# Attention and mixer on one core: the first channel product of two more chunks by seven half-size products, the last stores in more pieces, and every job in a new order

## The chip, the core and the metric

The kernel runs on one core of a Trainium2 chip. The core has five engines, each with its own queue of instructions: TensorE (PE in the profile, with PEld for its weight loads) for matrix products, VectorE (DVE) and ScalarE (ACT) for work on vectors, GpSimd (POOL), and SyncE (SP), which here only issues DMAs. Engines wait for each other through semaphores. The metric is device time in microseconds, the median of the runs; lower is better.

## The reference

`q`, `k` and `v` have 8 batch entries, 8 heads, 576 positions and head size 64. Linear attention with 128 random features gives `x`, and a token mixer and a channel mixer follow:

```python
def phi(x):                      # x: q or k, scaled by 64 ** -0.25
    proj = np.einsum('bhsd,md->bhsm', x, omega)
    h = proj - np.sum(x * x, axis=-1, keepdims=True) / 2.0
    h = h - np.max(h, axis=-1, keepdims=True)
    return np.exp(h) / np.sqrt(m)
q_p, k_p = phi(q_s), phi(k_s)
kv = np.einsum('bhsm,bhsd->bhmd', k_p, v);  z = np.sum(k_p, axis=2)
x = einsum('bhsm,bhmd->bhsd', q_p, kv) / (einsum('bhsm,bhm->bhs', q_p, z)[..., None] + 1e-06)
# x becomes [8, 576, 512]
h = np.maximum(x.transpose(0, 2, 1) @ w_tok1, 0.0) @ w_tok2     # 576 -> 256 -> 576
u = x + h.transpose(0, 2, 1)
out = u + np.maximum(u @ w_ch1, 0.0) @ w_ch2                    # 512 -> 1536 -> 512, float32
```

## The kernel before

A chunk is one batch entry's first 512 positions; chunks are numbered 0 to 7. The last 64 positions of all eight entries are gathered into a ninth chunk, number 8. Each chunk goes through three stages:

- `attention(b)`: products of the keys and queries with `omega` (lines 594 to 714), their exponentials on ACT (`exp`, line 557), row maxima of the keys on DVE (`km`, line 735), `v` scaled by their reciprocals (`vs_`, recorded at line 338), and two products with 65 columns (lines 758 and 791), whose result is divided and written to `x` (lines 807 and 809).
- `token_mix(b)`: two products (lines 826 and 839), the sum `u`, and a DMA on SP that transposes `u` into `uT` (line 847).
- `channel_mix(c)`: a first product with `wc1` and a rectifier into `r3` (tile `r`), then a second with `wc2`, added to `u` and stored.

The channel products are 512 by 512 by 1536. The second is done, from chunk 1 on, by `channel_out_fast`: both operands are cut in two by two blocks, and seven half-size products replace eight (products of block sums, put together again by additions). The block sums of `r3` go into tile `S`, those of the weights into `T`; the results are read out of the banks by `read` (line 964). The first is done in this way by `channel_in_fast` for the chunks from `FAST_IN` on: 4 to 8 here. For chunks below that, `channel_mix` runs 12 plain products of four matmuls of 512 columns (line 1167), each followed by a rectifier out of its bank.

In `channel_in_fast` each of three groups (`m`) has seven products of four matmuls of 256 columns (line 1096), P1 to P7. Three intermediate results are copied out of the banks (`keep`, ACT, recorded at line 329), three times DVE adds a kept copy to a bank (`join`, line 1120), and rectifiers follow: one out of a bank and two in place in SBUF. Four block differences of `uT` and eight sums of weights (`weight_sums`, once for the kernel) are needed as well. All sums can run on DVE or POOL.

The order of work is set by hand-held tables. Every piece of work is a job with a number, and `Planner.run` issues the jobs in the order of the list `ORDER` (a negative entry is a matmul on zeros that keeps the array busy). `SLOT` says which buffer of a ring each job takes, and `MOVED` on which engine a job runs where that isn't the usual one. An engine runs its own jobs strictly in that order. Between DVE and POOL, jobs marked `port` from attention chunk 2 on wait for the other engine's last such job (`Planner.turns`): the later one of a pair starts only after the earlier.

Keys and queries of chunks 2 to 7 are cast to half precision by POOL's DMAs into a scratch in DRAM, and then read back transposed by DMAs on SP (`load_transposed`, line 423). SP's queue also holds the transposes of `u` and many of the stores.

Of the kernel before, what the change touches and what calls it, by code (L numbers as in the profile page):

```python
# [208 lines left out]
def kernel(  # L209
# [12 lines left out]
    nc = tc.nc  # L222
# [3 lines left out]
    DM = H * D  # L226
# [8 lines left out]
    NCB = DC // P  # L235
    NU = H // 2
    R = SM // 2
    RT = ST // 2
    RA = R + RT
    NPE = 2  # L240
    FAST_IN = 4
    SPLIT = ()
    HALVES = ()
    RW = S * 4 // P
    c_scale = float(1.0 / math.sqrt(math.sqrt(D)))

    pool = ctx.enter_context(tc.tile_pool(name="sb", bufs=1))
# [1027 lines left out]
```

## Time and profile before

| | us |
|---|---|
| median of 3 runs (lowest, highest) | 272.78 (272.64, 273.68) |
| profiled execution, first to last instruction | 271.2 |
| PE busy, of that span | 262.6 (97%) |
| DVE busy | 225.1 (83%) |
| ACT busy | 167.4 (62%) |
| POOL busy | 149.9 (55%) |

The profiled execution has no other time of its own than its span; the median of the runs is 1.58 us above that span, which is what lies before the first and behind the last recorded instruction. The profile page shows busy time for each engine, the chain of work that ended last, and groups of instructions by source line. "L1167" is line 1167 of the kernel; `bank<-uT,wc` means that the instruction reads tiles `uT` and `wc` and writes a PSUM bank. Where a helper records the operation (lines 329 to 338), one line stands for many jobs, and the tiles tell them apart. Matmuls are pipelined, so the time of one is longer than the step from one to the next; the step is read from the chain, where so many matmuls fill so many microseconds.

### The profile page before, as it was taken

Reading aid. Unit: us, or ns where it says so; the run is one execution under the profiler, and the core shown is the slowest. Engines: PE = TensorE matmul, PEld = TensorE weight load, DVE = VectorE, ACT = ScalarE, POOL = GpSimd, SP = SyncE. Lnnn points to the kernel's source line nnn. Section 1 sums busy time; section 2 is a strip of 40 time slices with the busy share of each in tenths; the row PEclk is TensorE's granted clock in tenths of the full one; section 3 lists DMA queues with packets and bytes.
Section 4 is the critical chain, followed back from the end, with each engine's and each line's share of the span. In section 5 each row is a group of like instructions: output and inputs, shape, how many; then the busy total and the mean of one; then the engine's idle time right before and its main releaser. Section 6 shows DMA issues by size and latency. Waiting matters only on the chain.

```text
span 271.2 us, 6792 instructions
## 1 busy us (share of the span) xinstructions
PE 262.6 (97%) x2683; PEld 183.9 (68%) x2683; DVE 225.1 (83%) x483; ACT 167.4 (62%) x395; POOL 149.9 (55%) x155
## 2 busy tenths in 40 slices
PE   8899999999999999999999999999999999999992
PEld 4457455444557655775468687886698688888882
DVE  3888879759879779988888989989987986899882
ACT  2999942179683639637965989777768342482400
POOL 8895393066882694662898893692551025404041
PEclk9999999999999999999999999999999999999998
DMA  7999999998999999999846999701160182030026
GB/s 195 191 208 210 191 211 183 192 217 148 196 234 172 251 219 150 163 236 192 163 91 103 214 130 221 187 2 77 39 139 2 21 155 81 2 155 2 19 87 209
DMA packets 81297, 39.72 MB, mean 146 GB/s; under 512 B 63984, under 2 KB 77040, under 8 KB 81072
## 3 DMA queue, kind: packets, MB, share of 16 engines
q0 software_dynamic: 31744, 17.74, 44.1%
q1 hardware_dynamic: 46928, 15.37, 28.5%
q10 hardware_dynamic: 2592, 6.16, 6.0%
q8 instruction: 21, 0.34, 0.5%
q14 instruction: 12, 0.10, 0.1%
HBM read 35.95 MB, written 16.52 MB: 193 GB/s over the span
## 4 chain that ended last, share of the span: by engine, by line
PE 91%; ACT 3%; DMA 3%; DVE 1%; issue 0%
PE bank L984 27%; PE bank L1096 16%; PE bank L1167 15%; PE bank L826 5%; PE bank L839 5%; PE bank L1201 4%; PE bank L791 3%; PE bank L702 3%; PE bank L758 3%; DMA kT<-k 3%; PE bank L714 2%; PE bank L1241 1%; ACT kp L557 1%; PE bank L513 1%; PE bank L793 1%; PE bank L819 1%
## 5 line engine op out<-in xcount | busy, mean ns | idle before, releaser
L338 POOL TENSOR_TENSOR vs<-v,vs 128x512 f16<-128x512 f16 x31 | 32.7, 1060 | 24.4 <-DVE vs L739 9.6
L1167 PE MATMUL bank<-uT,wc 128*128 128x512 f16 x184 | 44.1, 379 | 0.0
L557 ACT ACTIVATE kp<-bank 128x512 f16<-128x512 f32 x64 | 34.9, 617 | 14.5 <-PE bank L702 14.5
L333 ACT ACTIVATE r<-bank 128x512 f16<-128x512 f32 (+1 forms) x52 | 30.6, 607 | 19.4 <-PE bank L1167 8.4
L984 PEld LDWEIGHTS <-r 128*128 128x128 f16 x384 | 36.6, 98 | 6.5 <-issue 1.9
L735 DVE TENSOR_REDUCE km<-kp 128x8 f16<-128x1024 f16 x32 | 38.2, 1203 | 2.3 <-ACT kp L557 2.3
L557 ACT ACTIVATE qp<-bank 128x512 f16<-128x512 f32 x64 | 35.6, 620 | 3.4 <-PE bank L714 3.4
L338 POOL TENSOR_TENSOR r<-r 128x768 f16<-128x768 f16 x9 | 14.7, 1641 | 33.7 <-DVE S L338 20.5
L984 PEld LDWEIGHTS <-S 128*128 128x128 f16 x288 | 27.7, 98 | 4.0 <-DVE S L338 0.3
L1167 PEld LDWEIGHTS <-wc 128*128 128x128 f16 x184 | 16.4, 97 | 16.7 <-issue 1.0
L984 PE MATMUL bank<-T,r 128*128 128x256 f16 x192 | 23.6, 273 | 0.0
L984 PE MATMUL bank<-T,S 128*128 128x256 f16 x192 | 23.6, 273 | 0.0
L984 PE MATMUL bank<-wc,r 128*128 128x256 f16 x192 | 23.3, 273 | 0.0
L807 ACT ACTIVATE x<-bank,rc 128x64 f16<-128x64 f32 x90 | 20.6, 353 | 4.3 <-DVE rc L798 2.9
L338 POOL TENSOR_TENSOR S<-r,S 128x768 f16<-128x768 f16 x10 | 16.3, 1644 | 11.8 <-DVE r L338 9.3
L809 DVE TENSOR_TENSOR x<-bank,rc 128x320 f16<-128x320 f32 x46 | 21.5, 482 | 0.8
L335 DVE TENSOR_SCALAR r<-bank 128x512 f16<-128x512 f32 (+1 forms) x29 | 19.0, 664 | 3.6 <-PE bank L1167 2.4
L964 DVE TENSOR_TENSOR o<-u,bank 128x512 f32<-128x512 f16 x28 | 18.9, 676 | 3.5 <-PE bank L984 3.4
L1096 PE MATMUL bank<-uT,wc 128*128 128x256 f16 x156 | 21.1, 273 | 0.0
L842 DVE TENSOR_TENSOR u<-x,bank 128x512 f16<-128x512 f16 x28 | 17.9, 682 | 2.2 <-PE bank L839 2.0
L1096 PEld LDWEIGHTS <-wc 128*128 128x128 f16 x180 | 17.1, 98 | 2.7
L791 PEld LDWEIGHTS <-qp 128*128 128x128 f16 x256 | 13.6, 98 | 4.2 <-issue 0.4
(157 smaller groups left out, 576.0 us busy)
## 6 DMA issues: line engine op xcount, KB each, us to landing
out_dram<-o ACTq DMA_DIRECT2D x9, 512.0 KB, 3.1
q<-in_q_dram POOLq DMA_DIRECT2D x6, 576.0 KB, 7.9
wc<-in_moe_w_ch_dram POOLq DMA_DIRECT2D x4, 768.0 KB, 10.6
k<-in_k_dram POOLq DMA_DIRECT2D x6, 512.0 KB, 8.1
v<-in_v_dram POOLq DMA_DIRECT2D x6, 512.0 KB, 8.0
out_dram<-o SPq DMA_DIRECT2D x5, 512.0 KB, 3.4
r<-in_q_dram POOLq DMA_DIRECT2D x4, 288.0 KB, 7.2
v<-in_v_dram POOLq DMA_DIRECT2D x4, 256.0 KB, 8.9
```

The source lines that it names most:

```text
L333: nc.scalar.activation(out=out, in_=in_, func=AF.Relu)
L335: nc.vector.tensor_relu(out=out, in_=in_)
L338: (nc.gpsimd if eng == "POOL" else nc.vector).tensor_tensor(**kw)
L557: nc.scalar.activation(out=out, in_=in_, func=AF.Exp, bias=0.0, scale=1.0)
L735: nc.vector.reduce_max(out=t_km[place("km", (b, hp))], in_=src_, axis=AX.X)
L791: nc.tensor.matmul(ps[:, k, j * 65 : (j + 1) * 65], st, s[:, i, 0 : D + 1], start=True, stop=True)
L807: nc.scalar.activation(out=to[:, j], in_=ps[:, j], func=AF.Copy, scale=rc[:, j : j + 1])
L809: nc.vector.tensor_tensor(out=to, in0=ps, in1=rc.unsqueeze(2).broadcast_to((P, NJ + 1, D)), op=ALU.mult)
L964: nc.vector.tensor_tensor(out=o, in0=a, in1=ps, op=ALU.add)
L984: nc.tensor.matmul(ps[:, j * DH : (j + 1) * DH], a[:, cb, j * P : (j + 1) * P], w[:, cb, :], start=(bank_of(b, j0) not in held and j == j0 ...
L1096: nc.tensor.matmul(ps[:, n, :], w(a)[:, (2 * m + n) * P : (2 * m + n + 1) * P], x_[:, a], start=(what in ("P1", "P2", "P5") and n == 0 and ...
L1167: nc.tensor.matmul(ps, wc1[:, db, cb * P : (cb + 1) * P], moving(db), start=(db == 0), stop=(db == ND - 1))
```

## The change

`FAST_IN` goes from 4 to 2, so the first channel product of chunks 2 and 3 also goes through `channel_in_fast`. For each of the two, 48 matmuls of 512 columns become 84 of 256. The second store of chunk 7 is cut into two column halves; in chunk 8 one store that covered both row halves is cut into two, and POOL is no longer fixed as its engine. `ORDER`, `SLOT` and `MOVED` are replaced throughout, and the entries -1 and below go from 16 to 11. The reading back of a transposed chunk and the cast that feeds it stand at places of their own in the new order. The code shifts by six lines from line 239 on, and by twelve at the end.

```diff
 ORDER = [
-    2, 5, 0, 6, 3, 1, 4, 16, 14, 18, 15, 7, 38, 12, -1, -2, -3, -4, -5, 39, 40, -6, 45, 9, 8, 47, 46, 10, 112, 41,
...
 MOVED = {
-    44: "ACT", 48: "ACT", 53: "ACT", 61: "ACT", 64: "ACT", 67: "ACT", 68: "ACT", 108: "ACT", 120: "DVE",
+    42: "DVE", 44: "ACT", 46: "ACT", 52: "ACT", 56: "ACT", 58: "ACT", 59: "ACT", 61: "ACT", 62: "ACT", 64: "ACT",
...
-    FAST_IN = 4
+    FAST_IN = 2
...
-            for i, js, cols, need in ((0, (0, 2), left, "11"), (1, (0, 2), right, "22"), (0, (0, 1), right, "12"), (0, (1, 2), right, "12"),
-                                      (1, (0, 1), left, "21"), (1, (1, 2), left, "21")):
+            for i, js, cols, need in ((0, (0, 2), left, "11"), (1, (0, 1), right, "22"), (1, (1, 2), right, "22"), (0, (0, 1), right, "12"),
+                                      (0, (1, 2), right, "12"), (1, (0, 1), left, "21"), (1, (1, 2), left, "21")):
                 for h in range(2):
-                    eng = engine("POOL" if need == "22" else "ACT" if h else "SP")
+                    eng = engine("ACT" if h else "SP")
...
-        for i, need in ((0, ["11", "12"]), (1, ["21", "22"])):
+        pieces = [(0, slice(0, DM), ["11", "12"])]
+        if c < B - 1:
+            pieces.append((1, slice(0, DM), ["21", "22"]))
+        else:
+            pieces += [(1, slice(DH, DM), ["22"]), (1, slice(0, DH), ["21"])]
+        for i, cols, need in pieces:
```

Three places show what the new tables do. The first is DVE where the first channel product of chunk 2 ends. Tile `r_129` is this chunk's `r3`, `x_118` the attention result of chunk 3, `qp` and `kp` here hold kept copies of banks. Before:

```order
L335 TENSOR_SCALAR r_129<-bank_65 128x512
L798 RECIPROCAL rc_147<-bank_69 128x5
L809 TENSOR_TENSOR x_118<-bank_67,rc_144 128x5x64
L809 TENSOR_TENSOR x_118<-bank_69,rc_147 128x5x64
L335 TENSOR_SCALAR r_129<-bank_70 128x512
L338 TENSOR_TENSOR S<-r_129 128x768 x2
```

And with the change:

```order
L1132 TENSOR_TENSOR r_129<-qp_95,bank_70 128x2x256
L815 TENSOR_TENSOR x_118<-bank_69,rc_147 128x5x64
L804 RECIPROCAL rc_146<-bank_63 128x5
L1132 TENSOR_TENSOR r_129<-kp_99,bank_65 128x2x256
L804 RECIPROCAL rc_148<-bank_64 128x5
L1132 TENSOR_TENSOR r_129<-kp_101,bank_70 128x2x256
L1132 TENSOR_TENSOR r_129<-kp_102,bank_69 128x2x256
L815 TENSOR_TENSOR x_118<-bank_64,rc_148 128x5x64
L1132 TENSOR_TENSOR r_129<-qp_97,bank_65 128x2x256
L1132 TENSOR_TENSOR r_129<-qp_98,bank_69 128x2x256
L341 TENSOR_SCALAR r_129<-r_129 128x1024 x2
L341 TENSOR_SCALAR r_129<-r_129 128x2x256
```

The rectifiers out of a bank have gone from DVE, and joins and rectifiers in place have come.

The second is POOL early in the program, where the weights of the first channel product (`wc_80`, two DMAs) are asked for. `vs` is the scaled `v` of chunk 0, `qpt` its last query positions, `vt` and `v_91` are loads for chunk 1. Before:

```order
L338 TENSOR_TENSOR vs_104<-v_90,vs_104 128x8x64
L676 COPY qpt_107<-qpt_107 128x8x64
L338 TENSOR_TENSOR vs_105<-v_90,vs_105 128x8x64
L468 DMA wc_80<-in_moe_w_ch_dram 128x4x768
L338 TENSOR_TENSOR vs_106<-v_90,vs_106 128x8x64
L468 DMA wc_80<-in_moe_w_ch_dram 128x4x768
L394 DMA vt_94<-in_v_dram 128x1x128
```

And with the change:

```order
L616 COPY T<-mask 128x16
L344 TENSOR_TENSOR T<-vt_93,mask 128x16x64
L368 DMA r_130<-in_q_dram 128x1152
L682 COPY qpt_107<-qpt_107 128x8x64
L474 DMA wc_80<-in_moe_w_ch_dram 128x4x768 x2
L386 DMA v_91<-in_v_dram 128x4x256
```

The three scalings of chunk 0 have left POOL for DVE, and both weight DMAs stand directly behind the copy.

The third is SP's queue from the keys of chunk 6 on: transposes of keys and queries (`kT`, `qT`), of `u` (`uT`, and `uTt` for chunk 8), and stores (`out_dram`). Before:

```order
L423 DMA_TRANSPOSE kT_89<-k_6_160 128x1x2304
L423 DMA_TRANSPOSE qT_86<-q_6_159 128x1x2304
L847 DMA_TRANSPOSE uT_127<-u_123 128x16x128
L847 DMA_TRANSPOSE uT_126<-u_124 128x16x128
L423 DMA_TRANSPOSE kT_88<-k_7_162 128x1x2304
L904 DMA_TRANSPOSE uTt<-ut 128x4x128 x2
L423 DMA_TRANSPOSE qT_85<-q_7_161 128x1x2304
L1026 DMA out_dram<-o_132 128x1024
L847 DMA_TRANSPOSE uT_128<-u_125 128x16x128
```

And with the change:

```order
L429 DMA_TRANSPOSE kT_89<-k_6_160 128x1x2304
L1037 DMA out_dram<-o_132 128x1024
L853 DMA_TRANSPOSE uT_128<-u_123 128x16x128
L429 DMA_TRANSPOSE qT_84<-q_6_159 128x1x2304
L429 DMA_TRANSPOSE kT_88<-k_7_162 128x1x2304
L1037 DMA out_dram<-o_132 128x1024
L853 DMA_TRANSPOSE uT_127<-u_124 128x16x128
L910 DMA_TRANSPOSE uTt<-ut 128x4x128
L429 DMA_TRANSPOSE qT_85<-q_7_161 128x1x2304
L1037 DMA out_dram<-o_131 128x1024 x2
L853 DMA_TRANSPOSE uT_128<-u_125 128x16x128
```

The keys of chunk 7 now stand ahead of the transpose of `u_124` (chunk 5) instead of behind it, and whole-tile stores stand between the transposes.

More of the change, by code (lines that the diff above doesn't have):

```diff
@@ L22 @@
 ORDER = [
[72 rows of a table removed]
[74 rows of a table added]
 ]
 SLOT = (
-    "0100234050600701103402521706330411560210401223120233033711614250603121274011353162700434056100673712"
-    "5604012137412011364072310230050171020343162253332400316147113252670150234273510456726122307162037060"
-    "2101403611743101500672132341016022340210153710060304721221311256200137405034166217310045360007231160"
-    "0514120035104163352201116013521130226023322300247231215031762225103506445703673205406111010711533212"
-    "1607431356207050146101037210023042621132416151237110114621370004437262522017230341625300127411073652"
@@ L102 @@
-    "7052306430302500224170306211134520211603340201152261201003530146001042170476635123150410171020302341"
-    "0713007123003024072311231042171200363451106172341125001274320451011005735620031131500035146134011672"
-    "3350140201372623547000632172523461301322524114020721020456357476031036732361103062040230607211045210"
-    "713221066004351206702201016412202076415102"
+    "0012340001506710102304526730113502400231231700613724236031152107016230021413350761345600571421363075"
+    "1415473110150427561321022320742151360030521473310641300110406257141022326015345466727220150100372011"
@@ new lines @@
+    "3007113700231627236113005170152067212313000460722023267051410124374211626451571372410630105116010032"
+    "0742012761433122020011137416201310207021320104722003641325016471222632711200051637700413211056700401"
+    "2376111010034176221127632103000332011210027114364015110031206113725122013670120500721112060621757132"
+    "3031756002230403532601710033760225013267220100151002413670113511230713052200101457602750040131760102"
+    "3610502170236102316572142150131756310027343250235101112114627511027450012016712716431450330620212034"
@@ L106 @@
+    "5551643700231401760120052461302530472123603021474561221351127036215546713001140711312472031311007420"
+    "11563035122230706450071020361120304672310561430120"
 )
 MOVED = {
-    44: "ACT", 48: "ACT", 53: "ACT", 61: "ACT", 64: "ACT", 67: "ACT", 68: "ACT", 108: "ACT", 120: "DVE",
-    122: "ACT", 128: "ACT", 139: "ACT", 147: "DVE", 149: "DVE", 153: "DVE", 157: "ACT", 159: "DVE", 167: "DVE",
-    171: "DVE", 173: "DVE", 175: "ACT", 179: "DVE", 185: "DVE", 191: "ACT", 197: "ACT", 207: "ACT", 208: "DVE",
@@ L111 @@
-    229: "ACT", 246: "ACT", 304: "DVE", 314: "DVE", 316: "DVE", 320: "DVE", 322: "DVE", 328: "POOL", 334: "POOL",
-    350: "ACT", 402: "ACT", 413: "DVE", 436: "ACT", 439: "DVE", 452: "DVE", 454: "DVE", 456: "DVE", 458: "DVE",
-    468: "DVE", 470: "DVE", 478: "POOL", 482: "POOL", 527: "DVE", 550: "ACT", 561: "DVE", 564: "ACT", 602: "DVE",
-    604: "DVE", 606: "DVE", 624: "DVE", 627: "POOL", 628: "POOL", 629: "POOL", 630: "POOL", 631: "POOL",
-    632: "POOL", 647: "ACT", 648: "ACT", 711: "DVE", 717: "ACT", 734: "ACT", 739: "DVE", 750: "POOL", 751: "POOL",
@@ L116 @@
-    752: "POOL", 753: "POOL", 756: "POOL", 757: "POOL", 758: "POOL", 760: "POOL", 809: "POOL", 810: "POOL",
-    812: "POOL", 814: "POOL", 816: "POOL", 831: "ACT", 861: "DVE", 878: "DVE", 898: "ACT", 901: "ACT",
-    936: "POOL", 937: "POOL", 938: "POOL", 952: "DVE", 953: "ACT", 954: "ACT", 970: "ACT", 987: "POOL",
-    988: "POOL", 992: "POOL", 1009: "ACT", 1039: "DVE", 1045: "ACT", 1059: "ACT", 1076: "ACT", 1093: "ACT",
-    1099: "DVE", 1101: "DVE", 1113: "POOL", 1145: "ACT", 1146: "ACT", 1162: "ACT", 1164: "POOL", 1168: "POOL",
@@ L121 @@
-    1185: "ACT", 1186: "ACT", 1235: "ACT", 1238: "ACT", 1252: "ACT", 1255: "ACT", 1289: "POOL", 1292: "POOL",
-    1324: "ACT", 1338: "DVE", 1342: "POOL", 1348: "POOL", 1363: "ACT", 1364: "ACT", 1371: "POOL", 1372: "POOL",
-    1404: "ACT", 1419: "ACT", 1420: "ACT", 1424: "POOL", 1428: "POOL",
+    42: "DVE", 44: "ACT", 46: "ACT", 52: "ACT", 56: "ACT", 58: "ACT", 59: "ACT", 61: "ACT", 62: "ACT", 64: "ACT",
+    65: "ACT", 86: "DVE", 103: "DVE", 120: "DVE", 122: "ACT", 137: "DVE", 139: "ACT", 142: "ACT", 147: "DVE",
@@ new lines @@
+    149: "DVE", 155: "DVE", 161: "ACT", 169: "DVE", 191: "ACT", 206: "ACT", 208: "DVE", 244: "DVE", 246: "ACT",
+    249: "ACT", 266: "ACT", 280: "DVE", 289: "DVE", 310: "DVE", 324: "DVE", 330: "POOL", 334: "POOL", 349: "ACT",
+    377: "DVE", 379: "DVE", 382: "ACT", 385: "ACT", 394: "DVE", 428: "DVE", 452: "POOL", 453: "POOL", 455: "POOL",
+    459: "POOL", 460: "POOL", 461: "POOL", 478: "ACT", 494: "ACT", 509: "ACT", 514: "POOL", 516: "POOL",
+    517: "POOL", 518: "POOL", 566: "ACT", 580: "DVE", 597: "DVE", 600: "ACT", 637: "POOL", 638: "POOL", 639: "POOL",
@@ new lines @@
+    640: "POOL", 688: "ACT", 690: "POOL", 692: "POOL", 694: "POOL", 696: "POOL", 744: "ACT", 764: "ACT", 781: "ACT",
+    798: "ACT", 813: "POOL", 814: "POOL", 815: "POOL", 816: "POOL", 832: "ACT", 848: "ACT", 868: "POOL",
+    869: "POOL", 870: "POOL", 872: "POOL", 887: "ACT", 920: "ACT", 923: "ACT", 940: "ACT", 991: "POOL", 992: "POOL",
+    993: "POOL", 994: "POOL", 1009: "ACT", 1010: "ACT", 1025: "ACT", 1026: "ACT", 1040: "DVE", 1042: "ACT",
+    1043: "POOL", 1044: "POOL", 1046: "POOL", 1048: "POOL", 1050: "POOL", 1066: "ACT", 1115: "ACT", 1118: "ACT",
@@ new lines @@
+    1129: "DVE", 1132: "ACT", 1157: "DVE", 1167: "POOL", 1168: "POOL", 1169: "POOL", 1174: "DVE", 1179: "DVE",
+    1190: "DVE", 1202: "ACT", 1209: "DVE", 1218: "ACT", 1221: "POOL", 1226: "POOL", 1271: "DVE", 1288: "DVE",
+    1291: "ACT", 1294: "ACT", 1308: "ACT", 1322: "DVE", 1328: "ACT", 1348: "POOL", 1364: "ACT", 1380: "ACT",
+    1395: "ACT", 1398: "POOL", 1399: "POOL", 1400: "POOL", 1401: "POOL", 1402: "POOL", 1403: "POOL", 1404: "POOL",
+    1421: "ACT", 1426: "POOL", 1427: "POOL", 1428: "POOL", 1429: "POOL", 1436: "DVE", 1444: "ACT", 1445: "ACT",
@@ L124 @@
+    1460: "ACT", 1461: "ACT", 1468: "DVE", 1470: "DVE", 1477: "ACT", 1480: "POOL", 1481: "POOL", 1485: "POOL",
+    1515: "SP", 1516: "POOL", 1517: "POOL", 1518: "ACT", 1519: "SP", 1520: "ACT", 1521: "SP", 1524: "ACT",
+    1525: "SP",
 }
@@ L1022, in channel_out_fast, with store @@
             return
-        for i, need in ((0, ["11", "12"]), (1, ["21", "22"])):
+        pieces = [(0, slice(0, DM), ["11", "12"])]
[4 more added lines that the diff above has]
+        for i, cols, need in pieces:
             eng = engine("SP")
-            def store(i=i, eng=eng):
-                (nc.scalar if eng == "ACT" else nc.sync).dma_start(out=out[c, 0:SM, :].rearrange("(p j) d -> p j d", j=NJ)[:, 2 * i : 2 * i + 2, :], in_=o_of(i))
+            def store(i=i, cols=cols, eng=eng):
+                (nc.scalar if eng == "ACT" else nc.sync).dma_start(
+                    out=out[c, 0:SM, :].rearrange("(p j) d -> p j d", j=NJ)[:, 2 * i : 2 * i + 2, cols], in_=o_of(i)[:, :, cols])
             dma(eng, key + 0.9 + 0.1 * i, 1.3, store, deps=[outs[x, 0] for x in need], give=[o_tag(i)], cost=0.4)
```

145 rows, old and new, of the table ORDER are left out of this document.

## The prediction

> **What bounds the kernel now.** I read the busy shares first, then the chain that ended last, then the waits of the engine that carries the chain, and last the stretches of the span in which the change works.
>
> ```profile
> span 271.2 us, 6792 instructions
> PE 262.6 (97%) x2683; PEld 183.9 (68%) x2683; DVE 225.1 (83%) x483; ACT 167.4 (62%) x395; POOL 149.9 (55%) x155
> PE 91%; ACT 3%; DMA 3%; DVE 1%; issue 0%
> ...
> PE bank L1241 <- DVE S L1238: 1.2, 1, 1.2
> PE bank L702 <- ACT kT L329: 0.7, 2, 0.5
> PE bank L594 <- DMA kT<-k: 0.6, 1, 0.6
> ```
>
> The chain is PE for 91% of the span, and PE's named waits are short; the one late in the kernel is 0.6 us for transposed keys. So the time is PE's work, plus a head in which little can run yet, plus a tail of stores.
>
> ```profile
> 0.00:20.00 20.00, 17.15 (x233) 9.79 (x234) 13.34 (x37) 14.62 (x37) 17.73 (x29) 1.00 1.06 198
> 20.00:40.00 20.00, 19.74 (x231) 12.13 (x224) 16.14 (x34) 16.75 (x39) 13.12 (x17) 1.00 1.27 203
> ...
> 160.00:180.00 20.00, 19.42 (x231) 16.44 (x230) 19.61 (x47) 15.82 (x43) 13.38 (x11) 1.00 0.77 153
> ...
> 260.00:272.00 12.00, 6.26 (x58) 5.35 (x55) 5.42 (x14) 0.00 (x0) 4.52 (x4) 0.90 0.44 133
> ...
> 60.00:140.00 80.00, 79.99 (x771) 48.13 (x768) 69.33 (x150) 56.03 (x134) 51.98 (x54) 1.00 1.11 190
> ```
>
> The columns after the length are busy time of PE, PEld, DVE, ACT and POOL, then the granted clock. Between 60 and 140 us, where the first channel products of chunks 2 and 3 lie, PE is busy for 79.99 of 80 us at full clock. DVE is busy for 69.33, ACT for 56.03, POOL for 51.98. In one stretch (160 to 180 us) DVE was busy for 19.61 of 20 us and PE still lost only the 0.58 that were free.
>
> **The products.** These pieces of the chain give the step of each kind of matmul:
>
> ```profile
> 92.12 5.18 PE bank L1167 x24
> ...
> 155.99 0.54 PE bank L1096 x4
> ...
> 235.24 8.73 PE bank L1096 x80
> ```
>
> 24 matmuls of 512 columns fill 5.18 us, 0.2158 each; 80 of 256 columns fill 8.73 us, 0.1091 each. Chunks 2 and 3 lose 2 x 48 = 96 of the first kind, 96 x 0.2158 = 20.72 us, and get 2 x 84 = 168 of the second, 168 x 0.1091 = 18.33 us. That is -2.39 us on the engine that sets the end. The 72 extra weight loads lie beside the matmuls: in the run of 80 each has one and the step is still close to half of 0.2158. If all new ones ran at the worst group above, 0.54 / 4 = 0.135 us, they would take 22.7 us, +2.0; I take -2.39 because long runs are the nearest rows to blocks of seven products.
>
> The Trainium skill, "TensorE: Matmul & The Clock Gate", section "Back-to-back issue gap", says that in a stream of weight loads and matmuls the spacing is set by both, about 81 ns at 128 columns and 131 ns at 512. On a straight line between these 256 columns would cost 98 ns, an estimate from that page, and 168 x 0.098 - 96 x 0.131 = +3.9 us: the change would lose. The trace disagrees, since its 512-column step is 216 ns where the page has 131; by the row the sum stays, and what is left of the rule is the last rival below.
>
> **What goes to the other engines.**
>
> ```profile
> 60.00:140.00 80.00, 11.51 (x17) 1.00 1.11 190
> ...
> 140.00:200.00 60.00, 11.81 (x18) 1.00 0.66 124
> L338 DVE TENSOR_TENSOR vs<-v,vs 128x512 f16<-128x512 f16 x1 | 0.6, 641 | 0.0
> L335 DVE TENSOR_SCALAR r<-r 128x1024 f16<-128x1024 f16 x12 | 4.8, 422 | 0.2
> L335 DVE TENSOR_SCALAR r<-r 128x512 f16<-128x512 f16 x8 | 2.3, 288 | 0.1
> L329 ACT COPY kp<-bank 128x512 f32<-128x512 f32 x15 | 8.9, 600 | 6.4 <-PE bank L1096 6.2 <-ACT kvsb L329 0.2
> L333 ACT ACTIVATE r<-bank 128x512 f16<-128x512 f32 x50 | 29.7, 613 | 19.4 <-PE bank L1167 8.4 <-PE bank L826 8.0 <-PE bank L1096 3.0
> L338 POOL TENSOR_TENSOR uT<-uT 128x512 f16<-128x512 f16 x4 | 4.6, 1162 | 6.7 <-DVE uT L338 6.7
> L338 POOL TENSOR_TENSOR S<-r,S 128x768 f16<-128x768 f16 x10 | 16.3, 1644 | 11.8 <-DVE r L338 9.3 <-DVE vbd L639 2.0 <-DVE S L338 0.5
> ```
>
> The first row is DVE's rectifiers (line 335) in that stretch, 17 for 11.51 us; the second is 18 joins (line 1120) later, 11.81 us. Going by the engines in the new tables, 14 of those rectifiers leave DVE in this stage (3 of chunk 1, 10 of chunks 2 and 3, 1 of token mixing): 14 x 0.677 = -9.5 us. There come 18 joins, +11.8; five rectifiers in place of 1024 columns at 4.8 / 12 = 0.40, +2.0; three of 512 at 0.29, +0.9; three scalings of chunk 2's `v` that POOL did, at 0.64, +1.9; one difference of `uT`, +0.4. DVE's stage goes from 69.3 to 76.8 us, while PE's shrinks from 80 to 77.6. That is 99%: free on paper, with almost no slack.
>
> ACT loses 14 rectifiers of chunks 2 and 3 (8.6 us by the 0.613 of the row), and there come 18 copies at 0.60 (10.8), 6 rectifiers out of banks (3.7), 4 in place (some 3) and the 4 that DVE gives up elsewhere (2.5): from 56.0 to about 67 of 77.6, covered. POOL gets 7 of the 8 new differences of `uT` at 1.16 and loses three scalings: about +5 on 52, covered too, if nobody on DVE waits for it. Over the whole kernel the block sums on POOL go up by 8 at 1.64 and those of `uT` by 12 at 1.16; each is a job that the next marked job on DVE waits for.
>
> What this costs PE is not shown by the trace. Below, nothing: DVE ran at 98% from 160 to 180 us and PE waited only for a DMA. Above, say half of DVE's idle time of the stage, (80 - 69.33) / 2 = 5.3 us, is forced and stays: 76.8 + 5.3 - 77.6 = 4.5 us. I take 0.7, near the lower end, because the 98% row is nearest to the new load but only a quarter as long.
>
> **The head.** The first full-size product of chunk 0 waits for weights and for a chain through ACT and DVE.
>
> ```profile
> 16.90 0.80 POOL L468 DMA_DIRECT2D wc<-in_moe_w_ch_dram  x1
> 17.72 1.07 POOL L338 TENSOR_TENSOR vs<-v,vs 128x512 f16<-128x512 f16 x1
> 18.72 0.80 POOL L468 DMA_DIRECT2D wc<-in_moe_w_ch_dram  x1
> DMA to landing us min/median/max: 9.0/10.6/12.3
> ...
> 29.57 0.81 PE L1173 MATMUL bank<-uT,wc 128*128 128x512 f16 x3
> ```
>
> The second weight DMA is issued at 18.72 and, by the landing row, is there by 31.0. Without the three scalings of 1.06 us on POOL both could be asked for 1 to 2 us sooner. The scalings cost DVE 3 x 0.64 = 1.9 us of the same chain instead. After the change two transposes of queries and three query products of chunk 1 stand behind the first products instead of ahead of them: they are moved, not saved. The identity matrix on POOL now stands behind four DMA issues. I bound the head by -1.4 (half of the 2.85 us in which PE idles before 20 us) and +1.0 (the scalings less what they gain), and take -0.3. The five dropped matmuls on zeros ran where PE had nothing else, so they cost nothing; the cover is that same idle time.
>
> **Transposes, stores, tail.**
>
> ```profile
> 162.69 7.32 DMA kT<-k
> ...
> DMA to landing us min/median/max: 4.5/5.4/7.3
> ...
> 266.29 0.42 DVE L964 TENSOR_TENSOR x<-x,bank 128x256 f32<-128x256 f32 x1 [0.23 <-PE bank L984]
> ```
>
> The 0.6 us wait ended with the keys of chunk 7, which took 7.32 us to land. In the new queue they stand ahead of the transpose of chunk 5's `u`, so this wait may go; ten whole-tile stores instead of five now stand in that queue between transposes, and one that waits for its tile holds up all behind it. I take 0 for the two together, between -0.6 and +2.8 (one transpose as much later as the slowest landing is over the fastest). ACT gives up six such stores, which frees some of its time. The tail is 271.2 - 266.7 = 4.5 us behind the last read; it again ends with one read and one pair of stores on SP and ACT, so 0. Cutting stores adds issues off that end.
>
> **Sum.** Against the profiled span: -2.39 + 0.7 - 0.3 + 0 = -2.0, so 269.2 us. The median of the runs is 272.78, 1.58 above the span, which gives 270.8 us. Half a percent, 1.36 us, is about what a measurement of this kernel can tell from no change: below 271.4 is faster, above 274.1 slower.
>
> **Rivals.**
> - *PE gains more.* The head takes its -1.4, DVE costs nothing and the key wait goes: 270.8 - 1.1 - 0.7 - 0.6 = 268.4 at the very best, about 269.5 if two of these three come. For it: all three are idle time that the page shows. Against it: the same tables would have to improve three places at once. Chance 0.10.
> - *A transposed operand comes late.* One store ahead of a transpose in SP's queue waits, and PE waits up to 2.8 us: 270.8 + 1.4 = 272.2 for half of it, up to 273.6. For it: the only late stall of before is of this kind. Against it: the order puts the keys earlier. This one gives the gain back without a net loss. Chance 0.18.
> - *DVE becomes the bound between 60 and 140 us, and the kernel gets slower.* PE can't reuse a bank that DVE hasn't read. With 76.8 us of work in 77.6, each microsecond beyond 0.8 in which DVE waits for an exchange with POOL or ACT is a microsecond of PE. At the 4.5 us above it ends at 270.8 - 0.7 + 4.5 = 274.6; the gain is gone from about 3.5 us of forced waiting on, and it counts as slower from 4.8. For it: DVE waited for POOL in several places before (1.3 us in a row like the one below), and POOL gets more sums, the slow ones at 1.64. Against it: jobs can spread into the 92% stretch behind. Chance 0.19, a bit over half of it slower.
> - *Small products don't run at half price* in the broken-up block: at 0.135 us each, 270.8 + 2.39 + 2.0 = 275.2. They pay below 20.72 / 168 = 0.123. Chance 0.03.
>
> ```profile
> DVE S L338 <- POOL r L338: 1.3, 1, 1.3
> ```
>
> The rule of the Trainium skill's "TensorE: Matmul & The Clock Gate" ("Back-to-back issue gap") would be the last of these rivals, at 270.8 + 2.39 + 3.9 = 277.1 by its two figures; its chance is within the 0.03, since the rows of both steps contradict it.
>
> **How the numbers follow.** My forecast has 0.50, from 270.0 to 271.6 us by its own small terms; nearly all of that is faster (0.47), a little within half a percent (0.03). With the first rival, faster gets 0.57. Within: 0.03 + 0.18 + 0.09 of the third, 0.30. Slower: 0.10 + 0.03 = 0.13. The range leaves out a tenth at each side: down to 269.0 for the first rival, up to 274.4, which takes in the late transpose and half of the DVE case.
>
> **What the profile after would show.** Line 1108 with 420 + 168 matmuls and long runs at 0.109 us; no 512-column channel products beyond chunks 0 and 1; PE's busy time down by about 2.4 us less what five matmuls on zeros change; DVE at or over 19 of 20 us between 60 and 140. I am wrong if PE's list of waits shows DVE's joins or reads in front of products in the microseconds, if a transposed `kT` or `uT` heads that list, or if the first full-size product starts more than 1 us after 29.57.

## The result and the profile after

The changed kernel takes 270.26 us (median of four runs, 269.62 to 271.26) against 272.96 for the kernel before; the ratio is 0.9886, with a 95% interval from 0.9845 to 0.9926. Measured once more later (`after_again`), the ratio was 0.9899, from 0.9863 to 0.9935. The gain is 2.7 to 3 us.

The profile page, with the span, the busy shares and the chain of the changed kernel, and its list of what PE waited for (total, times, longest):

```profile
span 268.5 us, 6991 instructions
PE 258.4 (96%) x2750; PEld 191.3 (71%) x2750; DVE 228.0 (85%) x483; ACT 185.6 (69%) x435; POOL 164.1 (61%) x165
PE 90%; DMA 3%; DVE 2%; ACT 2%; issue 1%; POOL 1%; SPq 0%; DVEq 0%; POOLq 0%
```

```profile
PE bank L519 <- POOL S masks.py:199: 4.3, 1, 4.3
PE bank L764 <- DVE vs L344: 0.7, 2, 0.5
PE bank L600 <- ACT kp L563: 0.3, 1, 0.3
PE bank L708 <- DMA kT<-k: 0.2, 1, 0.2
PE bank L670 <- DMA qT<-q: 0.2, 1, 0.2
```

The span is 2.7 us shorter (271.2 before), the run that this page shows took 270.25 us, 1.77 outside its span. PE still carries the chain. The first wait is the identity matrix for the first transposes; in the kernel before PE ran matmuls on zeros at that time, so it had no wait to show. Busy time by stage (PE, PEld, DVE, ACT, POOL, granted clock, DMA share):

```profile
0.00:20.00 20.00, 14.40 (x192) 9.08 (x194) 14.16 (x37) 13.68 (x31) 16.16 (x29) 1.00 1.08 197
20.00:40.00 20.00, 20.00 (x251) 11.97 (x242) 14.37 (x32) 18.05 (x41) 9.78 (x12) 1.00 1.23 206
...
60.00:140.00 80.00, 79.52 (x854) 56.70 (x853) 74.92 (x163) 67.60 (x165) 58.07 (x60) 1.00 1.20 194
...
120.00:140.00 20.00, 20.00 (x227) 15.20 (x226) 19.77 (x46) 19.85 (x54) 13.84 (x16) 1.00 1.13 199
```

Between 60 and 140 us DVE went from 69.33 to 74.92 us, ACT from 56.03 to 67.60 and POOL from 51.98 to 58.07, and PE was busy for 79.52 (79.99 before). In the last quarter of that stretch three engines are full at once: PE 20.00, ACT 19.85, DVE 19.77 of 20 us. The chain and the timeline give the steps:

```profile
100.12 3.06 PE bank L1108 x28
...
173.89 4.80 PE bank L1108 x44
```

```profile
28.45 1.90 PE L1179 MATMUL bank<-uT,wc 128*128 128x512 f16 x8
...
264.53 0.42 DVE L970 TENSOR_TENSOR x<-ut,bank 128x256 f32<-128x256 f16 x1 [0.23 <-PE bank L990]
```

In chunk 2 as in chunk 5 a 256-column matmul steps at 0.109 us (3.06 / 28, 4.80 / 44). The first full-size product starts 1.1 us earlier than before, but with less work done ahead of it. The last row is the last read of a bank: it starts 1.76 us earlier than before (266.29), and from there to the end of the span it is 3.95 us instead of 4.9. So the gain has two parts: 1.76 us up to the last read and 0.95 us behind it. `after_again` had its last read at 263.94 and its end at 267.9, which makes the two parts 2.35 and 0.95 us: its PE had neither of the two waits for transposed `kT` and `qT`.

### The profile page after: what moved, and what is told of

The parts are those of the page before. It is cut to its first block, busy times and chain, and to the rows that moved or that the text cites. A ratio compares the mean times of both kernels' runs of the same rounds, so it can differ in the third digit from the quotient of the medians.

```text
span 268.5 us, 6991 instructions
## 1 busy us (share of the span) xinstructions
PE 258.4 (96%) x2750; PEld 191.3 (71%) x2750; DVE 228.0 (85%) x483; ACT 185.6 (69%) x435; POOL 164.1 (61%) x165
## 4 chain that ended last, share of the span: by engine, by line
PE 90%; DMA 3%; DVE 2%; ACT 2%; issue 1%; POOL 1%; SPq 0%; DVEq 0%; POOLq 0%
PE bank L990 27%; PE bank L1108 24%; PE bank L1179 6%; PE bank L845 4%; PE bank L1213 4%; PE bank L832 4%; PE bank L708 3%; DMA kT<-k 3%; PE bank L764 3%; PE bank L797 3%; PE bank L720 3%; DVE km L741 1%; PE bank L899 1%; ACT kp L563 1%; PE bank L519 1%
## 5 line engine op out<-in xcount | busy, mean ns | idle before, releaser
L344 POOL TENSOR_TENSOR vs<-v,vs 128x512 f16<-128x512 f16 x24 | 25.3, 1056 | 9.8 <-DVE vs L745 4.4
L1108 PE MATMUL bank<-uT,wc 128*128 128x256 f16 x228 | 30.9, 273 | 0.0
L1108 PEld LDWEIGHTS <-wc 128*128 128x128 f16 x252 | 23.6, 98 | 3.5 <-issue 0.9
L813 ACT ACTIVATE x<-bank,rc 128x64 f16<-128x64 f32 x105 | 23.8, 348 | 2.6 <-DVE rc L804 2.6
L344 POOL TENSOR_TENSOR S<-r,S 128x768 f16<-128x768 f16 x15 | 24.4, 1642 | 0.1
L339 ACT ACTIVATE r<-r 128x512 f16<-128x512 f16 (+1 forms) x21 | 15.6, 756 | 11.0 <-DVE r L1132 10.8
L344 POOL TENSOR_TENSOR S<-S,r 128x768 f16<-128x768 f16 x5 | 8.2, 1641 | 22.4 <-DVE S L344 16.5
L1108 PE MATMUL bank<-uT,qT 128*128 128x256 f16 x126 | 21.7, 273 | 0.0
L1108 PE MATMUL bank<-uT,kT 128*128 128x256 f16 x126 | 21.1, 273 | 0.0
L1179 PE MATMUL bank<-uT,wc 128*128 128x512 f16 x88 | 21.0, 379 | 0.0
```

Source lines behind the costliest of these rows:

```text
L339: nc.scalar.activation(out=out, in_=in_, func=AF.Relu)
L344: (nc.gpsimd if eng == "POOL" else nc.vector).tensor_tensor(**kw)
L813: nc.scalar.activation(out=to[:, j], in_=ps[:, j], func=AF.Copy, scale=rc[:, j : j + 1])
L1108: nc.tensor.matmul(ps[:, n, :], w(a)[:, (2 * m + n) * P : (2 * m + n + 1) * P], x_[:, a], start=(what in ("P1", "P2", "P5") and n == 0 and ...
L1179: nc.tensor.matmul(ps, wc1[:, db, cb * P : (cb + 1) * P], moving(db), start=(db == 0), stop=(db == ND - 1))
```

## The experiments

There were three sets of four, each beside its own runs of the kernel before; ratios are compared between sets, times within one. An interval is about 0.3% to each side, so two kernels are told apart from about 1 us on; for less, the profile has to speak. "Changed" is `after_again`, 270.41 us.

> The changed kernel once more, as the measure for the runs beside it. 0.9886 of the kernel before in its first measurement; expected 0.986 to 0.993.

**Are the products worth their columns?** `plain_2_3` keeps the new order, but does the four plain products of each group where P1, P2, P5 and P7 stand:

```diff
+        PLAIN_OF = {"P1": ("X", lambda m: 2 * m), "P2": ("Y", lambda m: 2 * m + 1), "P5": ("Z", lambda m: NH + 2 * m), "P7": ("X", lambda m: NH + 2 * m + 1)}
...
+                    if c in PLAIN:
+                        if what in PLAIN_OF:
...
+                            for db in range(ND):
+                                nc.tensor.matmul(bank(bank_of(b, m)), wc1[:, db, cb * P : (cb + 1) * P], t_uT[place("uT", c)][:, :, db, :], start=(db == 0), stop=(db == ND - 1))
+                        return
```

> The changed kernel with its new order and stores, but with the first channel products of chunks 2 and 3 done as before: 96 matmuls of 512 columns with 24 rectifiers out of the banks, half of them on ACT and half on DVE, in the places of the small products, copies and joins. Theory 1, PE sets the end and the smaller products are worth their columns: +2.4 us against the changed kernel (2.39 by the two steps of before), so about the time of before. Theory 2, VectorE sets the pace between 90 and 140 us and eats the saving: DVE gets some 10 us lighter here, so +0.5 us or less, or even faster. Theory 3, the gain of the change comes from its order and its stores: 0 to +0.5 us.

It took 275.46 us, ratio 1.0079 (1.0047 to 1.0110): 5.0 us more than the changed kernel, twice what theory 1 said. In its list of waits PE waited for `x` in front of token mixing, because P3 and P4, which had covered the scaling of `x`, now held nothing:

```profile
PE bank L828 <- ACT x L816: 1.1, 1, 1.1
PE bank L767 <- DVE vs L347: 0.9, 2, 0.5
PE bank L828 <- DVE x L818: 0.5, 1, 0.5
```

`plain_spread` therefore puts the third product in two halves at P6 and P7 and the fourth at P3:

```diff
-        PLAIN_OF = {"P1": ("X", lambda m: 2 * m), "P2": ("Y", lambda m: 2 * m + 1), "P5": ("Z", lambda m: NH + 2 * m), "P7": ("X", lambda m: NH + 2 * m + 1)}
+        PLAIN_OF = {"P1": ("X", lambda m: 2 * m, (0, ND)), "P2": ("Y", lambda m: 2 * m + 1, (0, ND)), "P6": ("X", lambda m: NH + 2 * m, (0, 2)), "P7": ("X", lambda m: NH + 2 * m, (2, ND)),
+                    "P3": ("Z", lambda m: NH + 2 * m + 1, (0, ND))}
...
-                            for db in range(ND):
+                            for db in range(*dbs):
```

> Plain products in chunks 2 and 3 as in plain_2_3, which came out 5.0 us slower than the changed kernel, with PE waiting some 2.3 us for x ahead of two token-mix products. Here the same 96 matmuls are spread over other places (the third product in two halves where P6 and P7 stand, the fourth where P3 stands), so that PE has work while x is scaled. Theory 1 (the products are worth 2.4 us, the rest of the 5.0 was waits that came from where the work stood): +2.4 to +3.2 us against the changed kernel. Rival (the plain products cost about 5 us by themselves, for example through their rectifiers out of the banks): +4.5 us or more again.

273.84 us, ratio 1.0020 (0.9993 to 1.0047), 0.0121 above the changed kernel, 3.3 us; with both intervals that is anything from 2.1 to 4.5 us (an estimate). The rival of 4.5 us or more stands at the very edge of that: about a third of the 5.0 was waits that came from where the work stood. What is left is near the 2.4 us of the steps, with about 1 us of waits still in it (PE was busy for 19.45 of the 20 us from 120 on, and waited 0.4 us for a DVE rectifier and 0.3 for `kT`). Theory 3 is out as well: the order and the stores alone don't bring the gain.

**Is VectorE the bound?** `joins_quarter` shortens 12 of the 18 joins, `joins_twice` does nine of them twice:

```diff
+                    cols = slice(0, P // 2 if c in (2, 3) and i == 0 else 2 * P)
-                    nc.vector.tensor_tensor(out=r3(i, j, m), in0=kept(what, m).rearrange("p (n t) -> p n t", n=2), in1=pair(b, m), op=ALU.add)
+                    nc.vector.tensor_tensor(out=r3(i, j, m)[:, :, cols], in0=kept(what, m).rearrange("p (n t) -> p n t", n=2)[:, :, cols], in1=pair(b, m)[:, :, cols], op=ALU.add)
```

```diff
+                    for _ in range(2 if c == 3 else 1):
```

> The changed kernel with 12 of the 18 joins of chunks 2 and 3 done on a quarter of their columns (the rest of those outputs is left as it was), which takes about 12 x 0.45 = 5.4 us of work from DVE between 94 and 133 us and nothing else. Theory 1 (PE sets the end, DVE is just covered): -0.3 us to 0 against the changed kernel. Theory 2 (DVE sets the pace there): -0.7 us or more, up to -4; the 0.7 us that the prediction put down to DVE should come back.

> The changed kernel with the nine joins of chunk 3 done twice each, +9 x 0.68 = 6.1 us for DVE between 121 and 133 us, where it was busy for 19.77 of 20 us. Theory 1 in its strong form (DVE has room, since it can fall behind by some banks and catch up later in the 92% stretch): 0 to +1.5 us. Theory 2 (no room is left): +4 to +6 us.

With light joins 270.32 us (ratio 0.9891, 0.9866 to 0.9916): 0.1 us less than the changed kernel, so DVE's load costs PE nothing that this run can tell. With doubled ones 275.61 us (1.0079, 1.0053 to 1.0105): 5.2 of the added 6.1 us come through. The same stretch, 120 to 140 us, in both:

```profile
120.00:140.00 20.00, 20.00 (x228) 15.20 (x226) 17.93 (x45) 19.84 (x54) 13.85 (x16) 1.00 1.08 198
```

```profile
120.00:140.00 20.00, 16.23 (x195) 12.47 (x192) 19.62 (x43) 16.00 (x47) 11.08 (x13) 1.00 1.05 192
```

```profile
PE bank L1108 <- DVE r L1133: 2.2, 3, 1.1
```

In the first row (`joins_quarter`) DVE fell to 17.93 us and PE stayed at 20.00. In the second (`joins_twice`) DVE stayed full at 19.62 and PE fell to 16.23; the third, from its list of PE's waits, names the joins. So DVE stands just under the bound, with about 1 us of room. (A doubled join also frees its bank later; the run doesn't separate that from the load.)

**Would less PE work still pay?** `no_p7` leaves out P7 of the two chunks, `no_p7_light` also has the light joins:

```diff
+                    if what == "P7" and c in (2, 3):
+                        return
```

> The changed kernel without the 24 matmuls of P7 in chunks 2 and 3 (that product is left out of the sums; copies and joins stay). It takes 24 x 0.109 = 2.6 us from PE and nothing from the others. Theory 1 (PE alone sets the end, the others have room): -2.3 to -2.6 us. Theory 2 (VectorE stands right behind PE, so PE's saving would turn into waits for joins): -1 us to 0. The two other runs, with lighter joins 0.1 us faster and with doubled ones 5.2 us slower, speak for theory 2.

> Both at once: P7 of chunks 2 and 3 left out (24 matmuls, 2.6 us of PE) and 12 of their 18 joins on a quarter of the columns (5.4 us of DVE). Each alone left the time where it was (270.3 with light joins, 271.1 without P7, against 270.4 for the changed kernel). Theory 2 (between 90 and 150 us PE and VectorE stand level, so each alone gains nothing since the other takes over): now the saving shows, -1.5 to -2.6 us. Rival (without P7, PE waits for something that isn't DVE's load, for example the transposed u of chunk 4, which comes back at its own pace): about 271 again, -0.3 to +0.7.

Ratios 0.9917 (0.9885 to 0.9949) and 0.9907 (0.9876 to 0.9938): neither is faster than the changed kernel, and the 0.980 that 2.6 us less would give lies outside both intervals. The first result fitted theory 2; the second rules it out as the whole story, since with both PE and DVE lighter nothing was gained either. Where the saving goes shows in the starts of PE's token mixing (line 832) behind chunks 2 and 3, first in the changed kernel, then in `no_p7_light`, with the first product from the transposed `u` of chunk 4 as the last row:

```profile
103.77 1.04 PE L832 MATMUL bank<-x,w1m 128*128 128x512 f16 x4
133.19 1.04 PE L832 MATMUL bank<-x,w1m 128*128 128x512 f16 x4
```

```profile
102.45 1.90 PE L832 MATMUL bank<-x,w1m 128*128 128x512 f16 x8
132.19 1.04 PE L832 MATMUL bank<-x,w1m 128*128 128x512 f16 x4
148.57 0.61 PE L1110 MATMUL bank<-uT,wc 128*128 128x256 f16 x4 [0.51 <-DMA uT<-u]
```

At 103 us `no_p7_light` is 1.3 us ahead, which is all that the 12 matmuls of chunk 2 are worth. At 133 us it is 1.0 ahead, so chunk 3's saving has not come on top, and at 148.57 only 0.2 (the changed kernel starts that product at 148.74). The chain of `no_p7_light` shows where its critical work runs from 122 us on (start, length, what):

```profile
125.85 0.49 ACT r L335
126.34 0.50 ACT qp L563
126.84 0.20 ACT qp L335
...
130.04 1.28 ACT x L813 x5
131.32 0.50 ACT r L339
...
135.69 1.64 POOL r L344
137.33 1.02 POOL vs L344
138.35 0.77 POOL r L344
...
139.92 0.98 POOL vs L344
140.90 7.63 DMA uT<-u
```

From 122.6 to 131.9 us nearly all of it is ACT (copies of banks, exponentials, scalings), then PE's short products, then sums on POOL with which DVE takes turns, then the DMA that transposes chunk 4's `u`, 7.6 us. In the changed kernel ACT is full in the same place, and so is its neighbour DVE:

```profile
120.00:130.00 10.00, 10.00 (x128) 8.39 (x127) 9.78 (x24) 10.00 (x28) 6.00 (x7) 1.00 1.11 216
```

That ACT's ten full microseconds carry this second chain is read from the chain, not shown by a run: no kernel with a lighter ACT was tried.

**The tail.** `stores_as_before` takes back the pieces of the last stores, `store_late` sends chunk 7's second half as one store of 512 KB from ACT, later still:

```diff
-            pieces += [(1, slice(DH, DM), ["22"]), (1, slice(0, DH), ["21"])]
+            pieces += [(1, slice(0, 0), []), (1, slice(0, DM), ["21", "22"])]
...
-            for i, js, cols, need in ((0, (0, 2), left, "11"), (1, (0, 1), right, "22"), (1, (1, 2), right, "22"), (0, (0, 1), right, "12"),
+            for i, js, cols, need in ((0, (0, 2), left, "11"), (1, (0, 2), right, "22"), (1, (1, 1), right, "22"), (0, (0, 1), right, "12"),
```

An empty piece issues nothing. `store_late` has the first of the two edits, and job 1421, chunk 7's store, moves in `ORDER`:

```diff
-    1498, 1421, 1420, 1419, 1515, 1514, 1504, 1505, 1519, 1518, 1501, 1502, 1512, 1513, 1527, 1526, 1506, 1507,
+    1498, 1420, 1419, 1515, 1514, 1504, 1505, 1519, 1518, 1501, 1502, 1512, 1513, 1527, 1421, 1526, 1506, 1507,
```

> The changed kernel with the stores of before at the end: chunk 7's second half is one store of 512 KB behind its last read, and the two stores of chunk 8's right lower block cover both row halves each, issued by POOL. Order of everything else as changed. Theory A (the pieces shorten the tail): the span is 0.5 to 1 us longer, the stretch behind the last read goes from 3.5 to about 4.5 us. Theory B (the order did it, since chunk 7's last products now come 4 us earlier): 0 to +0.2 us.

> The changed kernel with chunk 7's second half as one store of 512 KB that ACT issues only behind its second store of chunk 8, at about 262 us, as late against the end as before the change. Theory B (what lengthened the tail was that 512 KB moved in the last microseconds together with chunk 8's stores): the stretch behind the last read grows from 3.5 to 4.3 to 5 us, the time by 0.7 to 1.5 us. If the tail is only the time of the very last small stores: 0.

Ratios 0.9920 (0.9889 to 0.9951) and 0.9948 (0.9922 to 0.9973), so 0.6 and 1.3 us over the changed kernel; the first interval overlaps with its, so the profile decides. The last reads of the two, each with its span:

```profile
core 0 of [0], span 269.9 us
...
265.32 0.42 DVE L970 TENSOR_TENSOR x<-ut,bank 128x256 f32<-128x256 f16 x1 [0.23 <-PE bank L990]
```

```profile
core 0 of [0], span 270.9 us
...
264.44 0.87 ACTq L1039 DMA_DIRECT2D out_dram<-o  x1
...
265.44 0.42 DVE L970 TENSOR_TENSOR x<-ut,bank 128x256 f32<-128x256 f16 x1 [0.23 <-PE bank L990]
```

From the last read to the end it is 4.6 and 5.5 us, against 3.95 in the changed kernel and 4.9 before. The pieces give 0.65 of the 0.95 us (theory A). The 0.3 that remain are not shown by a run; what still differs from before is the order, by which chunk 7's last store leaves at 259.27 instead of 262.97.

In `stores_as_before` that store had landed at 262.0, 3.3 us ahead of the last read, so it was no longer moving at the end. What is left there is chunk 8: two stores of 128 KB, at 263.40 and 264.04, where the changed kernel has four of 64 KB. ACT's 64 KB stores then took longer from issue to landing (the last number, a median); first the changed kernel, then `stores_as_before`:

```profile
out_dram<-x ACTq DMA_DIRECT2D x5, 64.0 KB, 2.3
out_dram<-x ACTq DMA_DIRECT2D x4, 64.0 KB, 3.5
```

A large store that leaves late costs more. In `store_late` it was issued at 264.44, 1.0 us ahead of the last read, and cost 1.5 us. Some 1.2 of these lie ahead of the last issue: ACT's queue issued its last store 1.85 us behind the start of the last read, in the changed kernel 0.65 us. What moved from about the last read on, by DMA share and GB/s at the row's end, before and after (the last reads are at 266.29 and 264.53):

```profile
266.00:268.00 2.00, 0.26 (x3) 0.00 (x0) 0.48 (x2) 0.00 (x0) 0.66 (x2) 1.00 0.89 236
268.00:270.00 2.00, 0.00 (x0) 0.00 (x0) 0.00 (x0) 0.00 (x0) 0.00 (x0) 0.88 0.54 154
```

```profile
264.00:266.00 2.00, 0.49 (x5) 0.20 (x2) 0.72 (x2) 0.00 (x0) 0.00 (x0) 1.00 0.77 212
266.00:268.00 2.00, 0.00 (x0) 0.00 (x0) 0.00 (x0) 0.00 (x0) 0.00 (x0) 1.00 0.29 84
```

```profile
262.97 0.86 ACTq L1026 DMA_DIRECT2D out_dram<-o  x1
```

The last row is chunk 7's last store before the change: it left 3.3 us ahead of the last read and landed at 266.4, so the first of the small stores ran together with it. `store_late` sends such a store 2.3 us later against the last read than that, so its 1.5 us are more than the one of before can have cost.

**The head.** `identity_first` and `head_early` differ from the changed kernel only in the first jobs of the list:

```diff
-    14, 7, 3, 2, 6, 12, 10, 22, 0, 4, 41, 15, 1, 38, 39, 42, 40, 16, 47, 48, 5, 78, 79, 80, 8, 11, 9, 13, 21, 19,
+    0, 14, 7, 3, 2, 6, 12, 10, 22, 4, 41, 15, 1, 38, 39, 42, 40, 16, 47, 48, 5, 78, 79, 80, 8, 11, 9, 13, 21, 19,
```

```diff
-    14, 7, 3, 2, 6, 12, 10, 22, 0, 4, 41, 15, 1, 38, 39, 42, 40, 16, 47, 48, 5, 78, 79, 80, 8, 11, 9, 13, 21, 19,
+    0, 14, 7, 3, 2, 6, 12, 10, 11, 22, 4, 41, 15, 1, 38, 39, 42, 40, 16, 47, 48, 5, 78, 79, 80, 8, 9, 13, 21, 19,
```

Job 0 makes the identity, job 11 asks for the first half of chunk 0's `v`.

> The changed kernel with the identity matrix made by POOL ahead of its four DMA issues instead of behind them; nothing else moved. The first transposes on PE waited until 4.30 us for it, against 3.84 us for their keys before the change. If the start of PE's first work sets the head: -0.3 to -0.45 us. If the head is set further on, by v and the exponentials, or if the four DMAs that are now asked 0.6 us later are wanted: 0 to +0.5.

> As identity_first, and the first half of chunk 0's v is also asked for before the second half of chunk 1's keys. In the changed kernel DVE waited 0.75 us, until 16.13, for that v, and PE then waited twice for the scaled v (1.0 us). If that wait carries the head: -0.6 to -1.0 us against the changed kernel, of it 0.5 or more beyond identity_first. If v is slow because the loads share the DMA engines (share over 1 throughout), asking earlier by 1 us brings less: 0 to -0.3 beyond identity_first.

Ratios 0.9894 (0.9869 to 0.9919) and 0.9925 (0.9897 to 0.9953): no gain, for the second rather a loss, though not beyond its interval. With the identity first, PE's first wait was 4.1 us, for the keys, instead of 4.3, and the gain came back as wait for `vs`:

```profile
PE bank L519 <- DMA wc<-in_k_dram: 4.1, 1, 4.1
PE bank L764 <- DVE vs L344: 1.5, 2, 1.0
```

The other kernel of the head drops the matmuls on zeros: every negative entry of `ORDER` is taken out.

> The changed kernel without its 11 matmuls on zeros (11 x 0.21 = 2.3 us of PE, in places of the head where PE has little else). If they only fill idle time: 0, within 0.3 us, as the prediction had it for the five that the change dropped. If some stand in the way of work that is ready: -0.2 to -1. If they hold the granted clock up: a lower clock in the first 40 us and up to +1 us.

272.16 us, ratio 0.9943 (0.9922 to 0.9965), some 1.2 us slower. A stretch in which several of the zeros had stood, and the one behind it, without them and then in the changed kernel:

```profile
12.20:15.60 3.40, 2.27 (x10) 0.68 (x10) 3.40 (x10) 3.40 (x10) 2.84 (x4) 0.97 1.30 202
15.60:22.20 6.60, 5.54 (x101) 5.08 (x102) 5.23 (x12) 4.63 (x13) 6.53 (x10) 0.50 1.18 204
```

```profile
12.20:15.60 3.40, 3.14 (x15) 0.98 (x14) 3.18 (x8) 3.40 (x11) 2.75 (x4) 1.00 1.31 200
15.60:22.20 6.60, 5.47 (x130) 4.33 (x129) 5.85 (x14) 5.53 (x14) 6.37 (x10) 1.00 1.18 204
```

Without the zeros PE was busy for 2.27 of 3.4 us instead of 3.14, and then the granted clock was 0.50 for 6.6 us, with 101 matmuls begun instead of 130.

None of these kernels was faster than the changed one by more than an interval.

## Why the prediction was right, point by point

The time came out 0.5 us under the forecast of 270.8, well inside the range. That it came so close is in part luck. VectorE's term (0.7 too dear) and the tail (0.95 not foreseen) both made the kernel faster than forecast, by 1.65 us together; the profiled span came out only 0.7 us under the forecast 269.2. By difference, the head and small waits in the middle came out some 0.95 us dearer than forecast and took back more than half of it.

- *Products, -2.39.* Right in mechanism and in size: the step in chunks 2 and 3 is 0.109 us. Counted from each start to the next on PE, the 96 matmuls that went had taken 20.97 us and the 168 that came take 18.33, 2.6 us less. `plain_spread` gave 3.3 us back, about 1 of it in waits. The rival of small products at 0.135 us is out by the same rows. The spacing rule of the Trainium skill ("TensorE: Matmul & The Clock Gate", "Back-to-back issue gap"), by which the change would have lost 3.9 us (an estimate from its figures), does not fit this case: the kernel gained 2.7.
- *VectorE's load, +0.7.* Mis-sized: it cost nothing measurable (`joins_quarter`, -0.1 us). Joins came as reckoned (18, about 12 us), the stage ended at 74.92 us rather than 76.8. The forced idle time of the upper bound did not come. But the rival was nearer than the result shows: of 6.1 us more, 5.2 came through.
- *ACT, "about 67 of 77.6, covered".* The total was right (67.60), the conclusion incomplete: a mean over 80 us hides that ACT is full from 120 to 130. The forecast had no row for a second chain through ACT, POOL and the transposing DMA; `no_p7_light` shows that something besides PE and DVE now stands level with PE, and its chain names this one.
- *Head, -0.3.* Of the wrong sign. The first full-size product came 1.1 us earlier (0.9 in `after_again`), but three query products, eight key matmuls and 18 transposes that had stood ahead of it now stand behind it. By the starts of the matmuls they take PE some 1.45 us there (an estimate from the two traces), so the head cost about 0.3 us in the profiled run and 0.6 in `after_again`; that is within the stated bounds. Earlier identity and `v` brought nothing. That the five dropped zeros are free is not shown, since no run puts them back. The clock row reads 1.00 for the first 20 us before and after, but the steps of the first transposes differ: before, 8 took 1.20 us from 6.44 on, in the profiled run 4 still took 1.01 us from 8.45 on. That this sets the head is unlikely: in `after_again` 4 took 0.66 us from 8.11 on, and its first full-size product came 0.25 us later. That zeros in general are free would have been wrong.
- *Transposes, 0.* Held within the stated bounds, but not nothing: the 0.6 us wait of before went. The two small ones of the profiled run, 0.2 us each by the list, came in its place; `after_again` had neither. There the 0.6 us gained is about what the head lost, so that its last read comes 2.35 us earlier, near to the 2.39 of the products, is no proof of that term by itself.
- *Tail, 0.* This step failed. "It again ends with one read and one pair of stores" was true, and the 4.5 us behind the end of that read still became 3.5. Taking the pieces back cost 0.65 of this 0.95 us (`stores_as_before`), and the small last stores then landed 3.5 us after their issue instead of 2.3. "Cutting stores adds issues off that end" looked at the issues and not at the bytes that are still moving.
- *What the profile would show.* Line 1108 has its new matmuls at 0.109, no join or read is in PE's list of waits, no transposed tile heads it. PE's busy time fell by 4.2 us, of which the dropped zeros are a part. "DVE at or over 19 of 20 us between 60 and 140" was wrong for its first half: 17.28 and 18.81 up to 100 us, then 19.06 and 19.77.

## What to carry to other kernels

When PE sets the end, a product with fewer columns gains about what its columns say, as long as the engines behind it have room in the very microseconds concerned: read their load in windows of 10 or 20 us, not over the stage, and count ACT as well as DVE. Once several engines are full in the same place, taking work from one of them (or, here, from two) need not show: follow the saving from stage to stage and see where it goes. At the end of a kernel, look at how many bytes are still moving when the last store is issued, and let the large stores leave early or in pieces.

## What the runs showed of the hardware

- In `no_zeros` the granted clock fell to 0.50 although PE was never idle for long: it was busy for 67% of 3.4 us, with one gap of 1.25 us, and the low clock then lasted 6.6 us. In the changed kernel, with 92% in the same stretch, it stayed at 1.00. The busy share alone doesn't tell when it falls: in `identity_first` PE was busy for 2.31 of 3.41 us (from 14.16 on), 68%, and the clock stayed at 1.00 there and behind. The Trainium skill, "TensorE: Matmul & The Clock Gate", section "What's actually happening", has the two clocks, full and half, and names an idle window of about 3.4 us as the reason for the lower one. The trace agrees on the half clock; here a window that was only partly idle was enough.
- The head of the changed kernel stands near that edge: in the profiles of `stores_as_before` and `joins_twice`, whose head is the same as in the changed kernel, the mean clock of the first 20 us was 0.95, as below (the last two columns before GB/s are clock and DMA share); in the other ten kernels that keep the zeros it was 1.00.

```profile
0.00:20.00 20.00, 13.77 (x160) 8.85 (x161) 13.96 (x34) 13.46 (x29) 15.46 (x28) 0.95 1.06 193
```

- The same transposing DMA of chunk 4's `u` took 7.6 us from issue to landing in `no_p7_light` and 6.2 in `after_again`, with the share of the DMA engines over 1 in both. What makes it vary stays open.
